# Gated linear unit behind a squared-ReLU attention: fetched and computed key pairs take turns, and v is loaded four key tiles at a time

## The chip, the cores and the metric

The kernel runs on one core of a Trainium2 chip. Its metric is the device time of one execution in microseconds: the median of three runs is 2310.55 us (2309.34 to 2316.06).

## The reference

Eight batches, 3200 rows, 256 columns of `u` and `v`, 64 columns of `z`, all in 32-bit floats.

```python
scores = (1 / S) * z @ z.T                      # per batch, 3200 x 3200
x = u * (maximum(scores, 0) ** 2 @ v)           # 3200 x 256
gate = sigmoid(sum over k < 5 of conv_w[k] * x shifted down by 4 - k rows)
out = (gate * (x @ w_val)) @ w_out
```

The score matrix is symmetric, since both of its factors are `z`. The kernel splits each factor of the large products into a high and a low part and adds three products (low by high, high by low, high by high).

## The kernel before, in words

A batch has 25 key tiles of 128 rows. They are taken in 13 pairs (the last is a single tile), and the queries in 7 chunks of 4, 4, 4, 4, 3, 3, 3 tiles (the last batch: 4, 4, 4, 4, 4, 3, 2). One chunk meets all 13 pairs, one a step; so there are 8 x 7 x 13 = 728 steps. A step at place p of its chunk does, in a fixed order written out by hand (the loop from L919):

- TensorE multiplies the pair's `ah` and `al` (high and low part of the squared scores, transposed) with `vt` into the chunk's two accumulators (`attend`, L552), and forms the scores of the pair three steps ahead (`scores`, L376). A pair product runs as two streams side by side in 64 rows each; where several steps in a row need no scores, it runs over all 128 rows (`attend_whole`, L561).
- The other engines run the work listed for that step (`todo`, filled by `at_step`), then `keep` (L437) sends finished transposes to memory, and `weights_of` (L468) makes the weights of the pair three steps ahead: on ScalarE Relu, Square and the cast to `ah`, on VectorE `al`, the difference.

**Mirrored pairs.** A pair whose scores are the transpose of scores already computed in an earlier chunk isn't computed again. When scores are computed, VectorE transposes them into `turned` (two buffers, L424), and SyncE stores a finished chunk-by-chunk block to memory (`mir`, L446, four transfers). Later `m_fetch` (L450) brings it back, three steps before its weights are made and six before TensorE uses it. Such a fetched pair needs no scores, no Relu, no Square and no transpose. Early chunks have few of them (none in chunk 0, two in chunk 1), late ones many (eleven in chunk 6). `MIRRORED_AT` (L249) says, by the number of fetched pairs in the chunk, which places they take; before, they stand mostly next to each other. A chunk's own second pair is half fetched and half computed and goes last. A pair that spans two query chunks needs two `turned` buffers at once; the last batch has no such pair in its chunks 0 and 1.

**v.** Batch 0 loads v as it goes. For later batches the v of pair i replaces the old one after the last chunk of the batch before has used it. With the step of that use as zero, SyncE issues the load at +3 (four transfers by partition quarter, eight where the pair spans two chunks), ScalarE casts the high part at +6, VectorE subtracts the low part at +7 (L903 to L907). So the last loads and casts fall into chunk 0 of the new batch. `v_raw` has five buffers of one pair, which `z_raw` shares.

**The tail of a chunk.** After place 12 VectorE multiplies the accumulators with `ut`, the transposed u (`gated`, L588; the instruction `x<-acc,ut`, L593). In the following chunk the list `BEHIND` (L823) runs the convolution, the sigmoid, the product with `w_val` (`value`, at step 5 or in pieces over steps that lack scores, L791) and the gating; one chunk later comes the product with `w_out` (`project`), the copies to `ob` and the store (L764). u is loaded by `u_load` (eight transfers a chunk) and transposed by `u_prep` (L582) at the steps of `U_LOAD` and `U_PREP`.

All loads and stores but a few stand in SyncE's queue, in program order: a transfer that must wait holds back all behind it. The same holds for the instructions of each other engine.

## Time and profile before

| | us |
|---|---|
| median of three runs | 2310.55 |
| profiled execution | 2313.36 |
| its span | 2311.6 |
| TensorE matmul busy | 2286.1 (99%) |
| TensorE weight loads busy | 2012.5 (87%) |
| VectorE busy | 1825.2 (79%) |
| ScalarE busy | 1771.8 (77%) |

In the profile PE is TensorE's matmul, PEld its weight load, DVE VectorE, ACT ScalarE, POOL GpSimd and SPq the queue of SyncE. Matmuls are pipelined and their ends are modelled, so a short wait of TensorE can vanish under the matmul before it; a window's length beside that of the same work elsewhere shows it all the same. "[3.62 <-DMA x]" behind a row is the idle time of its engine before it, and what ended it. L-numbers are lines of the kernel.

### The profile page before, as it was taken

What the parts mean: (1) busy time and instruction counts of PE and PEld (TensorE: products, weight loads), DVE (VectorE), ACT (ScalarE), POOL (GpSimd) and SP (SyncE); (2) the same over time, 40 slices, a digit from 0 to 9 for tenths busy, and PEclk for the clock granted to TensorE, in tenths of its full rate; (3) what the DMA queues carried; (4) which work ended last, traced back from release to release, by engine and by line L of the source; (5) the groups of instructions that cost most, each with busy time, mean ns of one, the idle gap of its engine ahead of it and who ended that gap; (6) DMA issues with size and microseconds to landing.
All of it is one profiled execution on the core that took longest, in us unless ns stands there. A gap on an engine that the chain in (4) does not pass through costs nothing.

```text
span 2311.6 us, 53404 instructions
## 1 busy us (share of the span) xinstructions
PE 2286.1 (99%) x21673; PEld 2012.5 (87%) x21673; DVE 1825.2 (79%) x2385; ACT 1771.8 (77%) x2400; POOL 65.5 (3%) x108
## 2 busy tenths in 40 slices
PE   9999999999999999999999999999999999999999
PEld 7889987889888898888988899888998889988889
DVE  7877788787877778887787877878788787888766
ACT  7987778866888668886688866887768877698765
POOL 0000000000000000000000000000000000000000
PEclk9999999999999999999999999999999999999999
DMA  5145676687667776676865777667776676767753
GB/s 123 38 106 129 149 166 149 163 198 191 161 150 170 185 199 158 146 179 167 210 161 138 197 164 198 157 147 197 165 191 153 159 193 156 198 159 189 185 147 101
DMA packets 659639, 375.02 MB, mean 162 GB/s; under 512 B 355520, under 2 KB 630976, under 8 KB 659392
## 3 DMA queue, kind: packets, MB, share of 16 engines
q1 hardware_dynamic: 658192, 371.35, 65.6%
q8 instruction: 169, 2.77, 0.5%
q14 instruction: 78, 0.64, 0.1%
q10 hardware_dynamic: 1200, 0.26, 0.1%
HBM read 205.86 MB, written 165.61 MB: 161 GB/s over the span
## 4 chain that ended last, share of the span: by engine, by line
PE 72%; SPq 7%; DMA 6%; ACT 6%; DVE 6%; issue 3%; DVEq 0%; ACTq 0%
PE acc L350 48%; PE misc L350 8%; PE s L350 7%; PE acc L563 7%; SPq L304 3%; DMA mir<-turned 3%; ACT a L516 2%; DVE al L525 2%; SPq L446 2%; ACT a L517 2%; DVE turned L424 2%; DMA v_raw<-in_v_dram 2%; SPq L168 1%; DMA m<-mir 1%; ACT ah L519 1%
## 5 line engine op out<-in xcount | busy, mean ns | idle before, releaser
L350 PE MATMUL acc<-ah,v_hl 64*128 64x512 f32 (+1 forms) x9656 | 1529.5, 371 | 4.2 <-DVE v_hl L337 3.5
L350 PEld LDWEIGHTS acc<-ah,v_hl 64*128 64x128 f32 x9656 | 907.0, 185 | 135.6 <-ACT ah L519 4.0
L350 PE MATMUL acc<-al,v_hl 64*128 64x512 f32 (+1 forms) x4828 | 911.5, 373 | 13.2 <-DVE al L525 12.6
L525 DVE TENSOR_TENSOR al<-a,ah 128x1024 fp32r<-128x1024 f32 (+3 forms) x387 | 423.1, 1094 | 222.1 <-ACT ah L519 213.2
L350 PEld LDWEIGHTS acc<-al,v_hl 64*128 64x128 f32 x4828 | 458.4, 185 | 90.6 <-DVE al L525 25.6
L525 DVE TENSOR_TENSOR al<-m,ah 128x768 fp32r<-128x768 f32 (+2 forms) x303 | 308.6, 1021 | 102.1 <-ACT ah L519 101.8
L516 ACT ACTIVATE a<-s 128x1024 f32<-128x1024 f32 (+3 forms) x387 | 355.3, 918 | 42.3 <-PE s L350 36.9
L519 ACT CAST ah<-m 128x768 fp32r<-128x768 f32 (+2 forms) x303 | 266.8, 893 | 153.3 <-DMA m<-mir 97.5
L517 ACT ACTIVATE a<-a 128x1024 f32<-128x1024 f32 (+3 forms) x387 | 371.2, 959 | 12.3
L424 DVE STREAM_TRANSPOSE turned<-a 128x1024 f32<-128x1024 f32 (+3 forms) x318 | 319.8, 1011 | 39.0 <-DMA mir<-turned 38.0
L519 ACT CAST ah<-a 128x1024 fp32r<-128x1024 f32 (+3 forms) x352 | 334.8, 951 | 11.2
L634 DVE SCALAR_TENSOR_TENSOR gate<-x,cw,gate 128x512 f32<-128x512 f32 (+2 forms) x448 | 305.2, 681 | 4.4 <-ACT gate L632 0.3
L350 PE MATMUL s<-zq,zhl 64*128 64x512 f32 (+3 forms) x1722 | 234.4, 373 | 1.3 <-ACT zq L231 1.3
L563 PE MATMUL acc<-ah,v_hl 128*128 128x384 f32 (+2 forms) x772 | 196.1, 332 | 0.2 <-DVE x L593 0.2
L350 PEld LDWEIGHTS s<-zq,zhl 64*128 64x128 f32 x1722 | 159.2, 185 | 26.7 <-ACT zq L231 1.6
L696 ACT CAST gvh<-gv 128x512 fp32r<-128x512 f32 (+2 forms) x112 | 64.2, 574 | 123.3 <-DVE gv L692 123.3
L639 ACT ACTIVATE gate<-gate 128x512 f32<-128x512 f32 (+2 forms) x112 | 65.5, 585 | 102.6 <-DVE gate L634 102.1
L563 PEld LDWEIGHTS acc<-ah,v_hl 128*128 128x128 f32 x772 | 137.8, 188 | 4.6 <-issue 1.5
L563 PE MATMUL acc<-al,v_hl 128*128 128x384 f32 (+2 forms) x386 | 127.7, 331 | 0.0
L350 PE MATMUL misc<-w_out_hi,gvl 64*128 64x256 f32 x676 | 98.3, 286 | 0.0
L593 DVE TENSOR_TENSOR x<-acc,ut 128x512 f32<-128x512 f32 (+2 forms) x112 | 65.9, 624 | 39.9 <-PE acc L350 26.2
L350 PE MATMUL misc<-w_out_hi,gvh 64*128 64x256 f32 x676 | 96.1, 279 | 0.0
(119 smaller groups left out, 2019.9 us busy)
## 6 DMA issues: line engine op xcount, KB each, us to landing
m<-mir SPq DMA_DIRECT2D x191, 384.0 KB, 4.7
mir<-turned SPq DMA_DIRECT2D x340, 192.0 KB, 3.5
mir<-turned SPq DMA_DIRECT2D x188, 256.0 KB, 4.3
m<-mir SPq DMA_DIRECT2D x94, 512.0 KB, 6.0
v_raw<-in_v_dram SPq DMA_DIRECT2D x328, 64.0 KB, 2.0
u_raw<-in_u_dram SPq DMA_DIRECT2D x264, 64.0 KB, 2.6
out_dram<-ob SPq DMA_DIRECT2D x33, 512.0 KB, 5.2
mir<-turned SPq DMA_DIRECT2D x84, 144.0 KB, 2.5
```

What stands on the lines that cost most here:

```text
L304: nc.sync.dma_start(dst[a * BLK : (a + 1) * BLK], v[b, k : k + m * BLK, :].rearrange("(t r) d -> r t d", r=BLK))
L350: ins = nc.tensor.matmul(out_, st[r], mv[r], start=first, stop=last)
L424: nc.vector.transpose(into[:, t : t + m], a[:, j * w : (j + m) * w].rearrange("p (t m x) -> p t m x", t=m, x=BLK))
L516: nc.scalar.activation(a.rearrange("p (j x) -> p j x", j=2), s[:, :, :each], AF.Relu, scale=scale)
L517: nc.scalar.activation(a, a, AF.Square)
L519: nc.scalar.copy(hi, a)
L525: nc.vector.tensor_tensor(lo, a, f32(hi), op=ALU.subtract)
L563: nc.tensor.matmul(out_, st, mv, start=first, stop=last)
L593: nc.vector.tensor_tensor(x[:, h, HALO : HALO + w], accs[b, c][h][:, :w], ut[b, c][:, h, :w], op=ALU.mult)
L634: nc.vector.scalar_tensor_tensor(g, tap, cw[:, h, k : k + 1], g, op0=ALU.mult, op1=ALU.add)
L639: nc.scalar.activation(g, g, AF.Sigmoid)
L696: nc.scalar.copy(gvs[b, c][0][:, e, :w], gv_[b, c, e][:, :w])
```

## The change

1. `MIRRORED_AT` puts fetched pairs at every second place where there are few of them, and one at place 1 where there are six, eight or nine. The last place of the chunk goes to a computed pair in three of these.
2. `VALUE_AT` names the places at which `value` is cut into pieces: none for two, four or six fetched pairs (there it runs whole at step 5), three or five places for the rest.
3. v of batches 1 to 7 is loaded in groups of four tiles at the steps of `V_LOAD`, counted from the start of the last chunk of the batch before, and cast at the steps of `V_HIGH` (low part one later). `v_raw` has two buffers of four tiles; `z_raw` has one of its own. A group that spans two chunks takes eight transfers, others four.
4. u of the first chunk is loaded at steps 6 to 9 instead of 2 to 5 and transposed at step 11 instead of 6; u of the second is loaded at steps 12 to 15 instead of 7 to 10, and transposed at 17 instead of 14; that of the third starts at step 18 instead of 15.
5. The small transposes (L434) of chunk 1's first pair go behind the two products `x<-acc,ut` of chunk 0.

```diff
     MIRRORED_AT = {
-        2: (8, 9),
-        4: (7, 8, 9, 10),
-        6: (4, 7, 8, 9, 10, 11),
+        2: (4, 8),
+        4: (4, 6, 8, 10),
+        6: (1, 4, 6, 8, 10, 12),
         7: (4, 5, 7, 8, 9, 10, 11),
-        8: tuple(range(4, 12)),
-        9: tuple(range(4, 13)),
+        8: (1, 4, 5, 6, 7, 8, 9, 11),
+        9: (1, 4, 5, 6, 7, 8, 9, 10, 11),
     }
...
+    def v_load(b, tiles, into=None):
+        raw = sb.tile([P, CW // P, D], F32, name="v_raw", bufs=2) if into is None else into
+        for j, k in enumerate(tiles):
+            v_raw[b, k] = raw, j
+        j = 0
+        while j < len(tiles):
+            g, t = all_homes[b][tiles[j]]
+            m = 1
+            while j + m < len(tiles) and all_homes[b][tiles[j + m]] == (g, t + m):
+                m += 1
+            v_rows(raw[:, j : j + m], b, g, t, m)
+            j += m
...
             if not mirrored(b, c, i):
+                if c == 1 and two_pairs(b, c) and i == own(b, c, 0) and place[b, c, i] == 0:
+                    return lambda: turn(b, c, i, a)
                 turn(b, c, i, a)
...
+    VALUE_AT = {2: (), 4: (), 6: (), 7: (4, 5, 6, 7, 8), 8: (4, 5, 6), 9: (4, 5, 6, 7, 8)}
...
-    U_LOAD = ((-6, -6, -11, -11, -11, -11, -6), (-6, -2, -2, -9, -11, -11, -6))
-    U_PREP = ((1,) * n_chunks, (10, 10, 3) + (1,) * (n_chunks - 3))
+    U_LOAD = ((6, -1, -8, -11, -11, -11, -6), (-6, -2, -2, -9, -11, -11, -6))
+    U_PREP = ((11, 4) + (1,) * (n_chunks - 2), (10, 10, 3) + (1,) * (n_chunks - 3))
+
+    V_LOAD = (
+        (
+            (-1, (0, 1, 2, 3)),
+            (1, (4, 5, 6, 7)),
+            (5, (22, 23)),
+            (7, (8, 9, 10, 11)),
+            (9, (12, 13, 14, 15)),
+            (12, (16, 17, 18, 19)),
+            (14, (20, 21, 24)),
+        ),
+        (
+            (-1, (0, 1, 2, 3)),
+            (1, (4, 5, 6, 7)),
+            (6, (8, 9, 10, 11)),
+            (8, (12, 13, 14, 15)),
+            (10, (16, 17, 18, 19)),
+            (12, (20, 21, 22, 23)),
+            (15, (24,)),
+        ),
+    )
+    V_HIGH = ((3, 4, 4, 6, 10, 11, 12, 13, 14, 15, 16, 8, 17), (3, 4, 5, 6, 8, 9, 10, 11, 12, 13, 14, 15, 17))
...
-            for i in range(NP):
-                free = start(b - 1, n_chunks - 1) + place[b - 1, n_chunks - 1, i]
-                at_step(free + 3, v_load, b, i)
-                at_step(free + 6, v_high, b, i)
-                at_step(free + 7, v_low, b, i)
+            s1 = start(b - 1, n_chunks - 1)
+            for i, p in enumerate(V_HIGH[b > 1]):
+                at_step(s1 + p, v_high, b, i)
+                at_step(s1 + p + 1, v_low, b, i)
+            for p, tiles in V_LOAD[b > 1]:
+                at_step(s1 + p, v_load, b, tiles)
...
                 if p != NP - 2:
-                    while held:
-                        held.pop(0)()
+                    for do in held[:]:
+                        held.remove(do)
+                        after = do()
+                        if after:
+                            held.append(after)
```

The first row of `V_LOAD` and `V_HIGH` is that of batch 1, the second that of batches 2 to 7.

More of the change, by code (lines that the diff above doesn't have):

```diff
@@ L155, in convert @@
         weights[name] = (hi, lo)
-    RAWS = 5
     zt = {}
@@ L177, in z_load @@
         else:
-            raw = sb.tile([P, CW // BLK, BLK], F32, name="z_raw", tag="v_raw", bufs=RAWS)
+            raw = sb.tile([P, CW // BLK, BLK], F32, name="z_raw", bufs=1)
         blocks_load(
@@ L296, in runs @@
         return out_
-    v_two = {}
     def v_rows(dst, b, g, t, m):
@@ L306, in v_rows, with v_load0 @@
             )
-    def by_chunk(b, i):
-        return b == 0 and all(2 <= g < 6 for _, g, _, _ in runs(b, i))
+    def v_load(b, tiles, into=None):
[10 more added lines that the diff above has]
+            j += m
+    two = {}
     def v_load_chunk(b, g):
         if g % 2 == 0:
-            v_two[b, g // 2] = sb.tile([P, 2, CW // P, D], F32, name="v_raws", tag="turned", bufs=2)
-        n = all_sizes[b][g]
-        v_rows(v_two[b, g // 2][:, g % 2, :n], b, g, 0, n)
-    def v_load(b, i):
-        raw = sb.tile([P, 2, D], F32, name="v_raw", bufs=RAWS)
-        v_raw[b, i] = raw
-        for j, g, t, m in runs(b, i):
-            v_rows(raw[:, j : j + m], b, g, t, m)
-    def v_parts(b, i):
-        if by_chunk(b, i):
-            return [(j, m, v_two[b, g // 2][:, g % 2, t : t + m]) for j, g, t, m in runs(b, i)]
-        return [(0, pairs[i][1], v_raw[b, i][:, : pairs[i][1]])]
+            two[0] = sb.tile([P, 2, CW // P, D], F32, name="v_raws", tag="turned", bufs=2)
+        v_load(b, range(all_firsts[b][g], all_firsts[b][g] + all_sizes[b][g]), two[0][:, g % 2])
+    def v_load0(k):
+        if k % 4 == 0 or k == 22:
+            two[1] = sb.tile([P, CW // P, D], F32, name="v_raw", bufs=2)
+        x = k // 2 % 2 if k < 22 else (k - 22) // 2
+        v_load(0, range(k, min(k + 2, NT)), two[1][:, 2 * x : 2 * x + 2])
+    def v_parts(b, i):
+        k, n = pairs[i]
+        if n == 2 and v_raw[b, k][0] is v_raw[b, k + 1][0] and v_raw[b, k][1] + 1 == v_raw[b, k + 1][1]:
+            raw, j = v_raw[b, k]
+            return [(0, 2, raw[:, j : j + 2])]
+        return [(x, 1, v_raw[b, k + x][0][:, v_raw[b, k + x][1] : v_raw[b, k + x][1] + 1]) for x in range(n)]
     def v_high(b, i):
@@ L789, in attn_glu_kernel @@
     }
+    VALUE_AT = {2: (), 4: (), 6: (), 7: (4, 5, 6, 7, 8), 8: (4, 5, 6), 9: (4, 5, 6, 7, 8)}
     def value_places(b, c):
-        s0 = start(b, c)
-        at_ = [p for p in range(4, 9) if lacks(s0 + p)] if (b, c) > (0, 1) and spread(b, c) else []
-        return at_ if len(at_) in PIECES else []
+        if (b, c) < (0, 2) or not spread(b, c):
+            return ()
+        return VALUE_AT.get(sum(mirrored(b, c, i) for i in range(NP)), ())
     def project_places(b, c):
@@ L806, in by_halves @@
         b, c, p = *chunk_of(s), s % NP
-        return p in value_places(b, c) or p in project_places(b, c)
+        return p in value_places(b, c) or p in project_places(b, c) or (p == VALUE and spread(b, c))
     todo = {}
@@ L897, in attn_glu_kernel @@
                 at_step(i - 2 if i else -3, v_low, b, i)
-                if not by_chunk(b, i):
-                    at_step(i - 5, v_load, b, i)
+            for k in (0, 2, 4, 6, 22, 24):
+                at_step(k // 2 - 5, v_load0, k)
             for g in range(2, 6):
@@ L1028, in attn_glu_kernel @@
         project_whole(b, c, spare=True)
-        for x, tag in enumerate(("zz", "v_raw")):
-            ob = sb.tile([P, CW // P * D // 2], F32, name="ob_half", tag=tag, bufs=(1, RAWS)[x])[:, : all_sizes[b][c] * D // 2]
+        for x, tag in enumerate(("zz", "z_raw")):
+            ob = sb.tile([P, CW // P * D // 2], F32, name="ob_half", tag=tag, bufs=1)[:, : all_sizes[b][c] * D // 2]
             (nc.scalar.copy, nc.vector.tensor_copy)[x](ob, pos[b, c][x][:, : all_sizes[b][c] * D // 2])
```

1 row of the table PIECES is left out of this document.

## The prediction

> **What bounds the kernel now.** I read the engine shares first, then the waits, then the busy time of TensorE in windows cut at the ends of chunks (where the first `x<-acc,ut` of a chunk starts).
>
> ```profile
> span 2311.6 us, 53404 instructions
> PE 2286.1 (99%) x21673; PEld 2012.5 (87%) x21673; DVE 1825.2 (79%) x2385; ACT 1771.8 (77%) x2400; POOL 65.5 (3%) x108
> ```
>
> The profiled execution took 2313.36 us, 1.8 us outside its span; the median of the runs, 2310.55 us, lies 2.8 us below it. TensorE is the bound, and the change leaves its work alone: counting through the plan, 303 of the 728 pair steps are fetched before and after, so the same score matmuls are left out, and 725 steps before the closing stretch hold 87 in the 128-row form instead of 93, with 15 changes of form both times. What can move is the time in which TensorE waits. Where that is shows in windows, each sum over seven batches (batches 1 to 7): chunk 0, chunk 1, chunk 4, chunks 5 and 6. After "us" come the window's length and TensorE's busy time in it.
>
> ```profile
> 1450.50:1499.40 48.90, 47.21 (x436) 38.78 (x434) 42.67 (x56) 43.88 (x57) 0.10 (x1) 1.00 0.68 166
> 2021.60:2068.40 46.80, 46.80 (x441) 39.16 (x440) 42.50 (x55) 42.97 (x56) 0.11 (x1) 1.00 0.68 167
> sum 336.60, PE 330.17 PEld 272.00 DVE 299.15 ACT 306.33 POOL 0.73; mean PE 47.17 PEld 38.86 DVE 42.74 ACT 43.76 POOL 0.10
> ...
> 1499.40:1546.90 47.50, 46.62 (x430) 38.12 (x428) 37.41 (x45) 39.53 (x49) 1.42 (x2) 1.00 0.60 148
> 2068.40:2113.80 45.40, 45.40 (x424) 37.88 (x422) 37.41 (x44) 40.61 (x50) 1.41 (x2) 1.00 0.62 155
> sum 329.90, PE 325.18 PEld 266.64 DVE 261.96 ACT 277.87 POOL 9.93; mean PE 46.45 PEld 38.09 DVE 37.42 ACT 39.70 POOL 1.42
> ...
> sum 247.00, PE 245.16 PEld 234.04 DVE 192.51 ACT 160.23 POOL 7.54; mean PE 35.02 PEld 33.44 DVE 27.50 ACT 22.89 POOL 1.08
> ...
> sum 450.70, PE 450.70 PEld 444.26 DVE 356.49 ACT 287.33 POOL 15.40; mean PE 64.39 PEld 63.47 DVE 50.93 ACT 41.05 POOL 2.20
> ```
>
> The last batch does the same matmuls in its chunks 0 and 1 without an idle moment, in 46.80 and 45.40 us. Against that the seven chunks 0 lose 336.60 - 7 x 46.80 = 9.0 us and the chunks 1 lose 329.90 - 7 x 45.40 = 12.1 us. Chunk 4 shows 247.00 - 245.16 = 1.8 us idle, chunks 5 and 6 none. The first batch adds two stalls, each with a drop of the granted clock (the column after POOL):
>
> ```profile
> 40.00:44.00 4.00, 1.34 (x10) 0.87 (x8) 3.23 (x8) 2.31 (x3) 0.00 (x0) 0.81 0.39 71
> 44.00:48.00 4.00, 4.00 (x20) 3.35 (x20) 4.00 (x9) 0.58 (x1) 0.00 (x0) 0.50 0.52 95
> 48.00:52.00 4.00, 4.00 (x35) 3.67 (x33) 1.69 (x5) 3.05 (x4) 0.00 (x0) 0.83 0.67 168
> ...
> 300.00:304.00 4.00, 2.68 (x18) 2.06 (x18) 1.77 (x4) 3.78 (x8) 0.00 (x0) 0.74 0.74 185
> 304.00:308.00 4.00, 4.00 (x40) 3.95 (x40) 3.73 (x7) 3.33 (x6) 0.00 (x0) 0.83 0.61 115
> ```
>
> The first costs 2.66 us of idleness, 4.00 x 0.50 = 2.0 at half clock and 4.00 x 0.17 = 0.7: 5.3 us. The second costs 1.32 + 2.68 x 0.26 + 4.00 x 0.17 = 2.7 us. So some 9.0 + 12.1 + 1.8 + 5.3 + 2.7 = 31 us could be had, and no more from these edits.
>
> **The change part by part.**
>
> **A, first u behind v.** This is the wait behind the stall at 43 us, and under it the transfers with their size and their time from issue to landing:
>
> ```profile
> 40.74 1.25 DVE L582 STREAM_TRANSPOSE ut<-u_raw 128x1024 f32<-128x1024 f32 x1 [3.62 <-DMA u_raw<-in_u_dram]
> ...
> v_raw<-in_v_dram SPq DMA_DIRECT2D x328, 64.0 KB, 2.0
> u_raw<-in_u_dram SPq DMA_DIRECT2D x264, 64.0 KB, 2.6
> v_raws<-in_v_dram SPq DMA_DIRECT2D x8, 128.0 KB, 2.9
> ```
>
> VectorE stood at step 6 for the u of chunk 0, and the v halves and `al` of steps 8 and 9 stood behind it. Now these eight u transfers are issued at steps 6 to 9, behind the v loads, and transposed at step 11; the product that reads them comes after step 12, so two steps of some 3.6 us (46.80 / 13) cover the landing of 2.6 us. Without that cover the wait would move in front of `x<-acc,ut`. I take 5.0 of the 5.3 us; ends 2.7 (the stall goes, the clock still drops) and 5.3.
>
> **B, v of batch 1 earlier.** In chunk 6 of the first batch ScalarE waits for v with the fetched casts queued behind it:
>
> ```profile
> 297.38 0.62 ACT L332 CAST v_hl<-v_raw 128x512 fp32r<-128x512 f32 x1 [3.61 <-DMA v_raw<-in_v_dram]
> ```
>
> The first eight v tiles are now issued at steps -1 and 1 of that chunk, and its last pair is computed, no longer fetched. I take 2.2 of 2.7; ends 0 and 2.7.
>
> **C, v of later batches by four tiles, cast two or three steps sooner.** Per batch 56 v issues become 36 (32 for the last), 288 instead of 432 in all. Chunk 0 of batch 5, SyncE's queue and then VectorE:
>
> ```profile
> 1456.62 5.50 SPq L304 DMA_DIRECT2D v_raw<-in_v_dram  x12
> 1462.21 3.02 SPq L446 DMA_DIRECT2D mir<-turned  x4
> 1465.34 3.14 SPq L304 DMA_DIRECT2D v_raw<-in_v_dram  x4
> 1468.58 0.41 SPq L764 DMA_DIRECT2D out_dram<-ob  x1
> 1469.03 2.75 SPq L304 DMA_DIRECT2D v_raw<-in_v_dram  x4
> 1471.82 4.18 SPq L446 DMA_DIRECT2D mir<-turned  x5
> ...
> 1468.62 1.25 DVE L424 STREAM_TRANSPOSE turned<-a 128x1024 f32<-128x1024 f32 x1 [1.26 <-DMA mir<-turned]
> 1478.38 1.25 DVE L424 STREAM_TRANSPOSE turned<-a 128x1024 f32<-128x1024 f32 x1 [1.88 <-DMA mir<-turned]
> ```
>
> SyncE issues without a pause; the stores of `turned` stand behind v, so their two buffers come free late, and VectorE loses 1.26 + 1.88 = 3.1 us there. An issue costs 5.50 / 12 = 0.46 us. In steps 12 to 15 there were 20 v issues, now 12: the stores go out 8 x 0.46 = 3.7 us sooner, more than the 3.1. Two of the six v casts that fell into chunk 0 move into chunk 6, where TensorE never idles: 2 x 0.618 = 1.2 us off ScalarE and about as much off VectorE.
>
> ```profile
> L332 ACT CAST v_hl<-v_raw 128x512 fp32r<-128x512 f32 x84 | 51.9, 618 | 39.1 <-DMA v_raw<-in_v_dram 39.1
> L516 ACT ACTIVATE a<-s 128x1024 f32<-128x1024 f32 x271 | 276.8, 1022 | 29.2 <-PE s L350 23.9 <-DVE turned L424 5.2
> L517 ACT ACTIVATE a<-a 128x1024 f32<-128x1024 f32 x271 | 287.7, 1062 | 8.6
> L424 DVE STREAM_TRANSPOSE turned<-a 128x1024 f32<-128x1024 f32 x179 | 221.8, 1239 | 20.7 <-DMA mir<-turned 20.5
> ```
>
> Of 9.0 I take 7; ends 2 (the casts alone) and 9.0.
> The Trainium skill (DMA: Bandwidth & Descriptors, section Issuing engines are not separate DMA queues) says that the time to start a transfer is usually small beside the transfer itself. By it the dropped issues would buy nothing, C would be 2 and the sum 14 instead of 19; here the trace disagrees, with twelve issues back to back in 5.50 us and a store waiting behind them.
>
> **D, fetched and computed alternate.** Chunk 1 of batch 5:
>
> ```profile
> 1513.81 1.24 DVE L424 STREAM_TRANSPOSE turned<-a 128x1024 f32<-128x1024 f32 x1
> 1523.96 0.71 DVE L424 STREAM_TRANSPOSE turned<-a 128x512 f32<-128x512 f32 x1 [2.97 <-DMA mir<-turned]
> 1526.01 1.22 DVE L525 TENSOR_TENSOR al<-a,ah 128x1024 fp32r<-128x1024 f32 x1
> ...
> 1516.04 0.41 SPq L764 DMA_DIRECT2D out_dram<-ob  x1
> 1516.49 3.58 SPq L446 DMA_DIRECT2D mir<-turned  x4
> ...
> PEld acc L350 <- DVE al L525: 1.7, 2, 1.3
> ```
>
> The pair that spans two chunks needs a second `turned` buffer, and that one is still on its way to memory; `al` of step 7 comes late, and in this chunk TensorE's weight loads wait for it twice, 1.7 us in all, 1.3 at most. The last batch has no such pair, and no loss. The buffer was full at 1513.81 + 1.24 = 1515.05 but was sent at 1516.49, behind the store of the output. With a fetched pair at place 4 instead of 9 the same three pairs are computed one step later: the store of the output is then already gone (1.4 us won), and before step 7 ScalarE has saved one Relu and Square (1.022 + 1.062 = 2.1 us) and VectorE one transpose (1.24). Together 2.6 us on VectorE against the 1.7. TensorE's work up to step 7 stays the same (five score groups before and after). Of 12.1 I take 8, since ScalarE has spare time only when VectorE is not behind; ends 0 and 12.1. In chunk 4 a fetched pair at place 1 relieves the step that idles: 1 of 1.8, ends 0 and 1.8. In chunks 2 and 3 the value matmuls go back from pieces into step 5, which lacks scores and so has room; nothing is won there, and a stall can appear: -1, ends 0 and -12.1 (as bad as chunk 1 now).
>
> **E, what the four-tile loads cost.** `v_raw` has two buffers of four tiles, so a load waits for the low parts of the previous owner, one step back or in the same step, and is cast two steps on, where it used to be three. Chunk 6 hides ScalarE's waits for v now (39.1 us in all, over seven batches), though not in batch 0. I take -3; ends 0 and 7 x 2.7 = -19. A transfer of 128 KB lands after 2.9 us, one of 64 KB after 2.0. `z_raw` gets a single buffer of its own; every load is at least as late as the transpose before it, so it goes with E.
>
> **F, small transposes behind the gate.**
>
> ```profile
> L434 DVE STREAM_TRANSPOSE turned<-a 128x256 f32<-128x256 f32 x60 | 22.9, 421 | 0.0
> ```
>
> Seven times two small transposes go behind `x<-acc,ut` at the start of chunk 1. The scores and the projection stand between that product and the next use of its banks, so I count nothing; if that cover were gone, they would save 7 x 2 x 0.421 = 5.9 us.
>
> The sum: 5.0 + 2.2 + 7 + 8 + 1 - 1 - 3 = 19.2 us. From the profiled 2313.4 that is 2294.2; from the median 2291.4 us. I forecast 2291.
> The Trainium skill (Perfetto Trace Analysis, section Identifying the Most-Contended Engine) judges TensorE's room by the share of weight loads, not of matmuls; at 87% that would leave 13%, or 299 us, where this text finds 31. The trace does not bear it out: chunk 1 of the last batch has TensorE busy for 45.40 of 45.40 us with weight loads at 37.88, or 83%.
>
> **The rivals.** *The loss moves on inside the chunk.* VectorE and ScalarE are busy for 42.67 and 43.88 us of chunk 0, so when one wait goes, the next step may be late instead. Then C and D give 2 each: 5.0 + 2.2 + 2 + 2 - 1 - 3 = 7.2 us, 2303. Against it stands the last batch, which carries the same work without idling. *No difference beyond the start.* The three pairs of D are still computed in successive steps, so the two buffers collide as before and the alternation doesn't do what it says; with C at its low end spent by E, 5.0 + 2 - 3 - 1 = 3 us, 2307.5. *Slower.* The four-tile loads come two steps ahead of their casts, with SyncE held by a VectorE that trails ScalarE. Where ScalarE then stands for v as long as the 3.61 us above, chunk 6 has no reserve left and TensorE stalls with a drop of the clock, 2.7 us in each of seven batches. That is -19, it uses up C and leaves 4 of D: 5.0 + 4 - 19 - 1 = -11, 2321.5. It decides from a wait of about 3 us per batch; against it, waits that summed to 39.1 us cost nothing in chunks 6.
>
> **How the numbers follow.** The forecast (gains of 9 to 33 us) 0.60; the loss moving on 0.20; no difference 0.12; slower 0.08. About 0.3%, 7 us, is what a measurement can tell from no change. Faster: 0.60 and, since the second case lies near that bound, 0.16 of its 0.20, together 0.76; same: the other 0.04 and the third case, 0.16; slower 0.08. All terms at their best give 5.3 + 2.7 + 9 + 12.1 + 1.8 = 31 us, 2279.6; the range adds a little for small gaps that no row shows, and reaches up past the third case: 2277 to 2308. The forecast's own bounds are 2277 to 2301.
>
> **What would show it.** Right: no 3.62 us wait of `ut` and a full clock from 44 to 52 us; chunks 0 and 1 of batches 1 to 6 at about 47 and 46 us; the wait of `turned` for its stores (38.0 us in total before) down by more than half; v issues 288. Wrong: idle time of TensorE in chunks 6, or a granted clock of 0.5 anywhere after the start (E); chunks 1 still at 47.5 us with the 3 us wait of `turned` in place (D); stalls in chunks 2 and 3.

## The result, and the profile after

The changed kernel takes 2289.97 us (median of four runs, 2285.6 to 2293.92) against 2311.76 us of the kernel before, measured beside it: a ratio of 0.9903, 95% interval 0.9878 to 0.9928. A second measurement gave 0.9892 (0.9878 to 0.9905). The forecast was 2291. The profiled execution took 2285.6 us and was the fastest of the four, so its gain of 27.8 us is larger than the 21.8 us of the medians.

The first lines of the page after, and then windows of the same kind as in the prediction: chunk 0 (batch 5, then the sum over batches 1 to 7), chunk 1 (batch 5, then the sum), chunk 4 (sum), chunks 5 and 6 together (sum).

```profile
span 2283.8 us, 53383 instructions
PE 2271.2 (99%) x21781; PEld 2034.1 (89%) x21781; DVE 1819.7 (80%) x2386; ACT 1774.3 (78%) x2399; POOL 65.9 (3%) x108
```

```profile
1431.20:1476.90 45.70, 44.98 (x413) 37.44 (x411) 40.71 (x52) 43.24 (x55) 0.10 (x1) 1.00 0.68 171
...
sum 319.50, PE 316.72 PEld 280.00 DVE 285.97 ACT 299.90 POOL 0.74; mean PE 45.25 PEld 40.00 DVE 40.85 ACT 42.84 POOL 0.11
...
1476.90:1522.80 45.90, 45.90 (x432) 38.34 (x430) 38.02 (x46) 41.10 (x51) 0.38 (x2) 1.00 0.70 157
sum 321.20, PE 321.20 PEld 272.02 DVE 265.71 ACT 285.05 POOL 2.68; mean PE 45.89 PEld 38.86 DVE 37.96 ACT 40.72 POOL 0.38
...
sum 245.00, PE 245.00 PEld 234.98 DVE 191.14 ACT 156.63 POOL 6.82; mean PE 35.00 PEld 33.57 DVE 27.31 ACT 22.38 POOL 0.97
...
sum 461.40, PE 460.73 PEld 451.28 DVE 360.94 ACT 296.77 POOL 17.67; mean PE 65.82 PEld 64.47 DVE 51.56 ACT 42.40 POOL 2.52
```

Chunks 1 went from 329.90 to 321.20 us and chunks 4 from 247.00 to 245.00, both now without an idle moment of TensorE. Chunks 0 went from 336.60 to 319.50, while chunks 5 and 6 grew from 450.70 to 461.40. That growth is mostly no loss. With the new places six score matmuls of each batch have moved, by way of the chunks between, from chunk 2 to chunk 5 (54 and 6 in the trace before, 48 and 12 after), about 1 us per batch. And `x<-acc,ut`, which ends a window, now comes late at the end of chunk 6, so that some of chunk 0's products count for chunk 6. For this reason the experiments below take chunk 6 together with the chunk 0 that follows.

The waits of the changed kernel (engine, line and what it waited for: us in total, times, longest):

```profile
ACT a L529 <- PE s L363: 130.9, 82, 4.3
ACT ah L532 <- DMA m<-mir: 54.9, 49, 4.5
ACT v_hl L345 <- DMA v_raw<-in_v_dram: 38.4, 39, 3.7
DVE turned L437 <- DMA mir<-turned: 5.9, 8, 1.7
PEld acc L363 <- DVE x L608: 4.8, 6, 1.8
```

The wait of `turned` for its stores fell from 38.0 to 5.9 us. ScalarE's wait for scores rose from 36.9 to 130.9, and the wait of TensorE's weight loads for `al` (L525, now L538) fell from 25.6 to 0.8: the other engines now wait for TensorE and no longer the other way round. But the wait of the v casts stayed (39.1, now 38.4), and a new wait of TensorE stands at the start of some chunks 0. This is the largest, at the start of the last batch (start, length, engine and line; in brackets the idle time before it):

```profile
1987.66 0.62 ACT L345 CAST v_hl<-v_raw 128x512 fp32r<-128x512 f32 x1 [1.53 <-DMA v_raw<-in_v_dram]
...
1993.79 0.69 DVE L534 CAST ah<-a 128x1024 fp32r<-128x1024 f32 x1
...
1994.39 1.02 DVE L608 TENSOR_TENSOR x<-acc,ut 128x384 f32<-128x384 f32 x2
...
1995.46 0.19 PEld L363 LDWEIGHTS acc<-ah,v_hl 64*128 64x128 f32 x2 [1.82 <-DVE x L608]
```

ScalarE waits 1.53 us for v in chunk 6, everything behind it comes later, VectorE's cast of `ah` stands ahead of `x`, and TensorE needs the accumulators that `x` sets free. In the first batch the stall at 302 us has only moved: TensorE now waits 2.3 us for `gvl` (the low part of the gated values, an operand of the product with `w_out`) at 304.95.

### The profile page after: what moved, and what is told of

It reads as the page before. It is cut to its first block, busy times and chain, and to the rows that moved or that the text cites. A ratio compares the mean times of both kernels' runs of the same rounds, so it can differ in the third digit from the quotient of the medians.

```text
span 2283.8 us, 53383 instructions
## 1 busy us (share of the span) xinstructions
PE 2271.2 (99%) x21781; PEld 2034.1 (89%) x21781; DVE 1819.7 (80%) x2386; ACT 1774.3 (78%) x2399; POOL 65.9 (3%) x108
## 4 chain that ended last, share of the span: by engine, by line
PE 92%; DMA 3%; DVE 2%; SPq 1%; ACT 1%; issue 1%; DVEq 0%; ACTq 0%
PE acc L363 65%; PE s L363 10%; PE misc L363 10%; PE acc L578 6%; DMA v_raw<-in_v_dram 2%; SPq L166 1%; DMA z_raw<-in_z_dram 1%; PE misc L749 1%; PE misc L694 1%; SPq L300 0%; DVE al L538 0%; ACT a L529 0%; ACT a L530 0%; DMA m<-mir 0%; DVE v_hl L350 0%
## 5 line engine op out<-in xcount | busy, mean ns | idle before, releaser
L363 PE MATMUL acc<-ah,v_hl 64*128 64x512 f32 (+1 forms) x9800 | 1552.7, 369 | 3.6 <-DVE x L608 3.3
L363 PEld LDWEIGHTS acc<-ah,v_hl 64*128 64x128 f32 x9800 | 937.5, 184 | 124.0 <-DVE x L608 4.8
L363 PE MATMUL acc<-al,v_hl 64*128 64x512 f32 (+1 forms) x4900 | 930.2, 369 | 0.2
L538 DVE TENSOR_TENSOR al<-a,ah 128x1024 fp32r<-128x1024 f32 (+3 forms) x387 | 423.1, 1094 | 253.8 <-ACT ah L532 246.6
L363 PEld LDWEIGHTS acc<-al,v_hl 64*128 64x128 f32 x4900 | 476.7, 184 | 57.0 <-DVE al L538 0.8
L529 ACT ACTIVATE a<-s 128x1024 f32<-128x1024 f32 (+3 forms) x387 | 355.4, 918 | 140.9 <-PE s L363 130.9
L532 ACT CAST ah<-m 128x768 fp32r<-128x768 f32 (+2 forms) x303 | 269.0, 893 | 111.3 <-DMA m<-mir 54.9
L538 DVE TENSOR_TENSOR al<-m,ah 128x768 fp32r<-128x768 f32 (+2 forms) x303 | 308.7, 1021 | 53.3 <-ACT ah L532 52.9
L363 PEld LDWEIGHTS s<-zq,zhl 64*128 64x128 f32 x1722 | 162.2, 184 | 21.3 <-ACT zq L229 0.4
L578 PE MATMUL acc<-ah,v_hl 128*128 128x384 f32 (+2 forms) x700 | 177.6, 331 | 0.2 <-DVE x L608 0.2
L578 PEld LDWEIGHTS acc<-ah,v_hl 128*128 128x128 f32 x700 | 124.7, 188 | 4.7 <-issue 1.1
L578 PE MATMUL acc<-al,v_hl 128*128 128x384 f32 (+2 forms) x350 | 115.5, 330 | 0.0
```

The lines of the kernel that those rows point to most:

```text
L363: ins = nc.tensor.matmul(out_, st[r], mv[r], start=first, stop=last)
L529: nc.scalar.activation(a.rearrange("p (j x) -> p j x", j=2), s[:, :, :each], AF.Relu, scale=scale)
L532: nc.scalar.copy(hi, a)
L538: nc.vector.tensor_tensor(lo, a, f32(hi), op=ALU.subtract)
L578: nc.tensor.matmul(out_, st, mv, start=first, stop=last)
```

## The experiments

All runs in one table. The second column is the difference of the median to the kernel before, measured on the same chip; the others are worked out from the profiled executions, as the time from the first `x<-acc,ut` of a chunk to that of the next: chunk 1 alone, and chunks 1 to 5, summed over batches 1 to 7; and chunk 6 with the chunk 0 behind it, summed over the seven places where they meet.

| kernel | to before, us | chunk 1 | chunks 1 to 5 | chunks 6 and 0 |
|---|---|---|---|---|
| before | 0 | 329.9 | 1415.3 | 587.2 |
| after | -21.8 | 321.2 | 1408.4 | 572.9 |
| after, once more | -25.3 | 321.2 | 1408.4 | 573.6 |
| old places | -10.3 | 335.5 | 1423.1 | 576.5 |
| old u | -17.4 | 321.2 | 1408.0 | 580.7 |
| old v | -19.1 | 321.2 | 1408.2 | 580.7 |
| new places in chunk 1 only | -20.9 | 321.2 | 1409.2 | 579.6 |
| fetched pairs side by side | -22.2 | 323.3 | 1410.2 | 576.3 |
| v by two tiles | -1.6 | 321.2 | 1408.0 | 598.4 |
| small transposes late in chunk 0 too | -6.9 | 321.2 | 1408.4 | 592.7 |
| small transposes all at once | -20.3 | 321.0 | 1408.3 | 581.5 |
| v by chunk | -22.4 | 321.6 | 1408.6 | 578.1 |
| v by chunk, a step later | -23.8 | 321.6 | 1408.5 | 575.7 |
| late transposes and later v | -19.2 | 321.2 | 1408.5 | 579.8 |

Two things can be read at once. Wherever chunk 1 has its new places, chunks 1 to 5 take 1408 to 1410 us, whatever else is changed. Among these kernels all other differences lie where chunk 6 meets chunk 0, apart from the first chunk of old u.

Two cautions go with the table. The profiled executions scatter at these meeting places: in the two of the changed kernel the first of them, behind the first batch, takes 83.3 and 86.4 us. And the windows are cut at `x<-acc,ut`, an instruction of VectorE, so they also measure how late VectorE is at the cut. TensorE's own first product with `w_out` in each chunk (`misc<-w_out_hi,gvl`) stands at a fixed place of its work. Cut there, the same sums are:

| kernel | chunk 1 | chunks 1 to 5 | chunks 6 and 0 |
|---|---|---|---|
| before | 330.3 | 1425.7 | 577.4 |
| after | 320.8 | 1411.5 | 570.3 |
| after, once more | 320.8 | 1411.6 | 571.0 |
| old places | 331.9 | 1429.3 | 570.7 |
| old v | 320.8 | 1411.4 | 578.1 |

The gain of all together is the same, but by this cut two thirds of it lie in chunks 1 to 5 and not where chunks 6 and 0 meet.

### The changed kernel again, and its three parts taken back

> The changed kernel once more, beside the three that take back one part each: 2290 us, some 21.8 us (0.94%) below the kernel before. It is the zero from which the three others are counted.

Measured: 2289.11 against 2314.43, 25.3 us less. The next three kernels ran on the same chip and are counted from it.

**Old places** (D).

```diff
-                at_ = MIRRORED_AT[len(fetched)]
+                at_ = (MIRRORED_AT if b == 0 and c == n_chunks - 1 else OLD_AT)[len(fetched)]
...
-    VALUE_AT = {2: (), 4: (), 6: (), 7: (4, 5, 6, 7, 8), 8: (4, 5, 6), 9: (4, 5, 6, 7, 8)}
+    VALUE_AT = {2: (5, 6), 4: (4, 5, 6, 7), 6: (4, 5, 6, 7, 8), 7: (4, 5, 6, 7, 8), 8: (4, 5, 6, 7, 8), 9: (4, 5, 6, 7, 8)}
```

> The changed kernel, but the fetched pairs stand at the old places and the value matmuls come in the old pieces (chunk 6 of the first batch alone keeps the new places). Theory (D, the alternation, is worth 8 us): 8 us slower than the changed kernel, 2298; chunks 1 of batches 1 to 6 take about 47 us instead of 45.9, and the waits of `turned` for its stores rise from 5.9 us towards 20. Rival 1 (the loss moves on, D gives 2 or less): within 2 us of the changed kernel, 2290 to 2292, chunks 1 at 46. Rival 2 (D carries nearly all of it, and C needs D): 15 us or more slower, 2305.

Measured: 2304.13 (ratio 0.9961, 0.9948 to 0.9973), 15.0 us above the changed kernel: the size of rival 2, though not its second half, that C needs D (below). The collision is there as the prediction told it. From its waits, its windows of chunk 1 (the sum), SyncE's queue and VectorE in chunk 1 of batch 5 (in one stretch of time):

```profile
DVE turned L446 <- DMA mir<-turned: 22.7, 16, 3.1
```

```profile
sum 335.40, PE 329.22 PEld 271.61 DVE 266.07 ACT 274.99 POOL 2.65; mean PE 47.03 PEld 38.80 DVE 38.01 ACT 39.28 POOL 0.38
```

```profile
1508.87 0.41 SPq L788 DMA_DIRECT2D out_dram<-ob  x1
1509.32 3.56 SPq L468 DMA_DIRECT2D mir<-turned  x4
...
1516.57 0.71 DVE L446 STREAM_TRANSPOSE turned<-a 128x512 f32<-128x512 f32 x1 [2.74 <-DMA mir<-turned]
```

The first buffer goes out behind the store of the output, and the transpose of the spanning pair waits 2.74 us for it. Chunks 1 take 335.4 us here, 5.5 us more than in the kernel before, but most of that is the cut. These are TensorE's first product with `w_out` and VectorE's `x` at the start of chunk 1 of batch 5, in the kernel before and then here:

```profile
1498.59 0.28 PE L350 MATMUL misc<-w_out_hi,gvl 64*128 64x256 f32 x2
1499.38 1.25 DVE L593 TENSOR_TENSOR x<-acc,ut 128x512 f32<-128x512 f32 x2
...
1491.08 0.28 PE L372 MATMUL misc<-w_out_hi,gvl 64*128 64x256 f32 x2
1491.28 1.29 DVE L617 TENSOR_TENSOR x<-acc,ut 128x512 f32<-128x512 f32 x2
```

VectorE comes to `x` 0.79 us after TensorE's product before, and 0.20 us here, so the window opens sooner. Cut at TensorE's product, chunks 1 differ by 1.6 us (330.3 and 331.9) and chunks 1 to 5 by 3.6, in one profile of each. So at most a part of what the new v gains is passed on as a loss, and the collision costs about what it cost before.

**Old u** (A).

```diff
-    U_LOAD = ((6, -1, -8, -11, -11, -11, -6), (-6, -2, -2, -9, -11, -11, -6))
-    U_PREP = ((11, 4) + (1,) * (n_chunks - 2), (10, 10, 3) + (1,) * (n_chunks - 3))
+    U_LOAD = ((-6, -6, -11, -11, -11, -11, -6), (-6, -2, -2, -9, -11, -11, -6))
+    U_PREP = ((1,) * n_chunks, (10, 10, 3) + (1,) * (n_chunks - 3))
```

> The changed kernel, but the u of the first chunk is fetched and transposed at the old steps. Theory (A is worth 5.0 us): 5 us slower than the changed kernel, 2295; `ut` waits about 3.6 us for `u_raw` near 41 us, TensorE idles 2.7 us there and the granted clock falls to 0.5 behind it. Rival 1 (the idle time goes, the clock would have fallen anyway, A = 2.7): 2 to 3 us slower. Rival 2 (the new v loads alone move the wait away, since fewer issues stand behind u): no difference over 1 us and no wait of `ut`.

Measured: 2297.03 (0.993, 0.9917 to 0.9943), 7.9 us above. VectorE, TensorE's weight loads, then windows of this kernel, and then windows of the changed kernel:

```profile
40.45 1.25 DVE L597 STREAM_TRANSPOSE ut<-u_raw 128x1024 f32<-128x1024 f32 x1 [3.35 <-DMA v_raw<-in_v_dram]
...
42.85 0.22 PEld L363 LDWEIGHTS acc<-ah,v_hl 64*128 64x128 f32 x2 [2.70 <-ACT ah L532]
```

```profile
44.00:46.00 2.00, 2.00 (x13) 1.76 (x11) 2.00 (x7) 0.00 (x0) 0.00 (x0) 0.50 0.40 81
46.00:48.00 2.00, 2.00 (x15) 1.80 (x13) 1.97 (x5) 1.73 (x2) 0.00 (x0) 0.66 0.76 127
```

```profile
40.00:44.00 4.00, 4.00 (x40) 3.23 (x37) 3.27 (x8) 3.66 (x5) 0.00 (x0) 1.00 0.51 100
44.00:48.00 4.00, 4.00 (x42) 3.35 (x39) 2.97 (x8) 3.75 (x5) 0.00 (x0) 1.00 0.30 111
```

The wait of `ut` is back (the row names a transfer of v as what ended it, not u), and with it the stall and the half clock. The first chunk ends 4.0 us later (at 60.3 instead of 56.3 us). That is what A is worth in its place. The other 3.9 us lie where chunks 6 and 0 meet (580.7 against 573.6), in code that is the same in both kernels. There the kernel with all small transposes at once (581.5) is as far from the changed one, and both profiles have a drop of the clock (at 1160 and at 874 us) that neither profile of the changed kernel has. The intervals of the two ratios leave room for a difference as small as 2.8 us. Whether A acts that far isn't shown.

**Old v** (B, C, E).

```diff
-        raw = sb.tile([P, CW // P, D], F32, name="v_raw", bufs=2) if into is None else into
+        raw = sb.tile([P, 2, D], F32, name="v_raw", bufs=RAWS)
...
-            for p, tiles in V_LOAD[b > 1]:
-                at_step(s1 + p, v_load, b, tiles)
+                at_step(free + 3, v_load, b, i)
+                at_step(free + 6, v_high, b, i)
+                at_step(free + 7, v_low, b, i)
```

> The changed kernel, but v of every batch is fetched, cast and split pair by pair at the old steps, with five buffers of two tiles. Theory (B 2.2 + C 7 - E 3): 6 us slower than the changed kernel, 2296; `turned` waits again for its stores for over 20 us in all, chunks 0 of batches 1 to 6 take about 47.5 us instead of 45.6, and TensorE idles 1.3 us again near 302 us. Rival 1 (E eats C, as the wait of the v casts is still 38.4 us): within 2 us, with the stalls of TensorE at the start of chunks 0 of batches 3, 5 and 7 (1.15, 0.88, 1.77 us) gone. Rival 2 (v carries most of the gain): 12 us or more slower.

Measured: 2295.31 (0.9918, 0.9904 to 0.9931), 6.2 us above, as the terms had it. Three of its waits:

```profile
ACT v_hl L332 <- DMA v_raw<-in_v_dram: 37.9, 31, 3.1
ACT ah L519 <- DMA m<-mir: 36.3, 21, 3.5
DVE turned L424 <- DMA mir<-turned: 19.4, 17, 2.4
```

The waits of `turned` are 13.5 us longer than in the changed kernel, TensorE's weight loads wait 11.8 us for `al` (0.8 and 2.6 in the two profiles of the changed kernel), and chunks 0 take 334.3 instead of 319.4 us: C is real. But the wait of the v casts is the same with either scheme (37.9 and 38.4). What the new scheme makes longer is the wait of `ah` for the fetched `m`, from 36.3 to 54.9 us, as the v loads now stand between the fetches of chunk 6. Chunks 6 take 253.5 instead of 246.4 us to the late `x` at their end. TensorE itself loses nothing inside them: from its first product with `w_out` to that of the next chunk, chunks 6 of batches 1 to 6 take 33.5 us each in the kernel before, in this one and in the changed one. E is paid at the start of chunk 0, where TensorE's weight loads wait for `x`: 1.4 us in all here, 4.8 and 2.3 in the two profiles of the changed kernel. At the end of batch 0 this kernel's weight loads wait 1.4 us for `gvl` and 1.2 us for `x`, the changed kernel's 2.3 us for `gvl`.

### What of D counts

**New places in chunk 1 only.** The kernel with the old places, but its rows for two fetched pairs are the new ones.

```diff
     OLD_AT = {
-        2: (8, 9),
+        2: (4, 8),
...
-    VALUE_AT = {2: (5, 6), 4: (4, 5, 6, 7), 6: (4, 5, 6, 7, 8), 7: (4, 5, 6, 7, 8), 8: (4, 5, 6, 7, 8), 9: (4, 5, 6, 7, 8)}
+    VALUE_AT = {2: (), 4: (4, 5, 6, 7), 6: (4, 5, 6, 7, 8), 7: (4, 5, 6, 7, 8), 8: (4, 5, 6, 7, 8), 9: (4, 5, 6, 7, 8)}
```

> The kernel with the old places (2304.1 us, 15.0 us over the changed kernel), but chunk 1 alone has its two fetched pairs at the new places 4 and 8 and its value matmuls whole. Theory (what D is worth lies in chunk 1): the seven chunks 1 come back from 48.2 to 45.9 us, 7 x 2.3 = 16 us less some for the start of chunk 2, so 10 to 15 us faster than with the old places, 2289 to 2294. Rival (the backlog is handed from chunk to chunk, and chunks 2 to 4 need the new places too): chunks 1 at 46, but chunks 2 and 4 lose a microsecond each, 7 us or less won, 2297 or more.

Measured: 2291.87, 20.9 us below before (0.9906, 0.9894 to 0.9919), 1 to 4 us above the changed kernel, which can't be told from nothing. Chunks 1 are at 45.9 us. Chunks 2 and 4 take 5.1 and 2.8 us more than in the changed kernel, but chunk 5 takes 6.5 us less, since the scores stay where they were. Of the 15.0 us of D, chunk 1 alone brings 10.6 back (from 10.3 to 20.9 us below before).

**Fetched pairs side by side.**

```diff
     MIRRORED_AT = {
-        2: (4, 8),
+        2: (4, 5),
```

> The changed kernel, but the two fetched pairs of chunk 1 stand side by side at places 4 and 5 instead of 4 and 8. Theory of the prediction (what counts is one fetched pair at place 4, so that the pair that spans two chunks comes when its buffer is free): within 2 us of the changed kernel, 2289 to 2291, chunks 1 at 45.9 to 46.1. Rival (what counts is that no more than three computed pairs stand in a row, so that ScalarE and VectorE catch up): seven computed pairs in a row from place 6 run late, chunks 1 at 47 to 48, 7 to 14 us slower, 2296 to 2303.

Measured: 2290.57, 22.2 us below before (0.9902, 0.9889 to 0.9915), the same as the changed kernel; `turned` waits 4.2 us for its stores, chunks 1 take 46.2 us. So it isn't the alternation. One fetched pair at place 4 and one right behind it are enough, ahead of the pair that spans two chunks.

### What of v counts

**v by two tiles.**

```diff
-            while j + m < len(tiles) and all_homes[b][tiles[j + m]] == (g, t + m):
+            while m < (2 if b else 4) and j + m < len(tiles) and all_homes[b][tiles[j + m]] == (g, t + m):
```

> The changed kernel, but the v of batches 1 to 7 is fetched by at most two tiles in one transfer, at the same steps into the same buffers: 52 to 56 issues per batch instead of 36. Theory (an issue holds SyncE's queue for 0.46 us, and the stores of `turned` stand behind it): the waits of `turned` for its stores rise from 5.9 us to 15 or more, chunks 0 take half a microsecond to one more, 3 to 7 us slower, 2292 to 2296. Rival 1, by the rule that the time to start a transfer is small beside the transfer: within 1 us, 2289 to 2290. Rival 2 (the long landing of 4.4 us of a four-tile transfer is what makes ScalarE wait for v): the waits of the v casts fall from 38 us to 20, the stalls at the start of the chunks 0 go, 2 us faster.

Measured: 2311.25, 1.6 us below before (0.9992, 0.9983 to 1.0): 20 us or more slower than the changed kernel, far beyond all three expectations. SyncE's queue in chunk 6 of batch 2 (the number at the end counts the issues), ScalarE, the waits, and the sum of the windows of chunk 6 (236.30 in the changed kernel); then SyncE's queue of the changed kernel at the same place:

```profile
838.13 1.21 SPq L474 DMA_DIRECT2D m<-mir  x2
839.39 5.27 SPq L300 DMA_DIRECT2D v_raw<-in_v_dram  x8
844.76 1.77 SPq L474 DMA_DIRECT2D m<-mir  x2
846.59 4.84 SPq L300 DMA_DIRECT2D v_raw<-in_v_dram  x8
...
859.76 0.83 ACT L532 CAST ah<-m 128x768 fp32r<-128x768 f32 x1 [2.93 <-DMA m<-mir]
```

```profile
ACT ah L532 <- DMA m<-mir: 84.0, 52, 3.5
DVE turned L437 <- DMA mir<-turned: 2.7, 5, 1.2
```

```profile
sum 254.30, PE 243.10 PEld 232.79 DVE 197.90 ACT 154.59 POOL 9.47; mean PE 34.73 PEld 33.26 DVE 28.27 ACT 22.08 POOL 1.35
```

```profile
834.48 1.21 SPq L474 DMA_DIRECT2D m<-mir  x2
835.74 2.04 SPq L300 DMA_DIRECT2D v_raw<-in_v_dram  x4
837.88 1.20 SPq L474 DMA_DIRECT2D m<-mir  x2
839.12 2.62 SPq L300 DMA_DIRECT2D v_raw<-in_v_dram  x4
```

The issue is the price, as the theory had it, but not where it had it: `turned` waits less than in the changed kernel, and it is the fetches of `m` between the v loads of chunk 6 that come late, 84.0 instead of 54.9 us of waits, and TensorE idles there and at the start of chunk 0. There the clock takes a part of the 20 us. At the starts of chunks 0 of batches 4 to 7 the granted clock falls to one half for 3.41 us, which neither profile of the changed kernel shows; this is the first of the four:

```profile
1162.56:1165.97 3.41, 3.41 (x20) 2.74 (x18) 3.38 (x5) 3.08 (x6) 0.00 (x0) 0.50 0.48 110
```

Four of them are 4 x 3.41 x 0.50 = 6.8 us of TensorE's work. The same two-tile transfers at the old steps (old v) cost 6 us; at the new steps they cost 20. Without the larger transfers the earlier steps would have eaten nearly the whole gain.
The Trainium skill (DMA: Bandwidth & Descriptors, section Issuing engines are not separate DMA queues) calls the time to start a transfer usually small beside the transfer itself; by it this run would have shown no difference. The trace doesn't agree: the same bytes in 144 transfers more took 20 us longer, with eight issues holding the queue for 5.27 us ahead of a fetch.

**v by chunk, and a step later.** In batches 2 to 6 no load spans two chunks: 28 issues instead of 36. In the second kernel the last two loads and their casts come a step later, behind the first stores of chunk 0 (the last lines of the diff).

```diff
+    BY_CHUNK = (
...
+        (10, (16, 17, 18)),
+        (12, (19, 20, 21)),
+        (15, (22, 23, 24)),
+    )
...
-        (12, (19, 20, 21)),
-        (15, (22, 23, 24)),
+        (13, (19, 20, 21)),
+        (16, (22, 23, 24)),
```

> The changed kernel, but in batches 2 to 6 the last three loads of v hold the tiles 16 to 18, 19 to 21 and 22 to 24, so that none spans two chunks: 28 issues per batch instead of 36, eight fewer behind the fetches of chunk 6, at the same steps. Theory (each issue less on SyncE's queue brings the fetches of `m` and the stores of `turned` forward; 20 more of them cost 20 us over seven batches, 0.14 us each): up to 40 x 0.14 = 5.7 us faster, I expect 1 to 5, 2284 to 2288; the waits of `ah` for `m` fall below 50 us and the stalls at the starts of chunks 0 halve. Rival 1 (the price of an issue is only seen above some number of them): within 1 us. Rival 2 (three transfers of three tiles need the v buffers later than before, and casts come a step later): slower by 1 us or more.

> As the kernel before in this list, but the last two loads come one step later, behind the first stores of `turned` of chunk 0 instead of ahead of them, with their casts one step later too. Theory (the order of stores and v loads on SyncE's queue decides, as where the delayed small transposes put the stores behind v and lost 15 us): the stores of the first pairs of chunk 0 go out some 2 us sooner; `turned` waits less than 5.9 us in all; 0 to 2 us faster than with the earlier steps. Rival (the casts that move into chunk 0 take ScalarE's spare time there): chunks 0 at 46 to 47 us instead of 45.6, 2 to 8 us slower.

Measured: 22.4 us (0.9904, 0.9887 to 0.992) and 23.8 us (0.9902, 0.9884 to 0.9919) below before. Both are the changed kernel's time. In the second the waits of `turned` fall to 1.1 us, but those of `ah` for `m` stay at 56.8. Eight issues fewer per batch buy nothing, where some 20 more per batch cost 20 us: from 36 issues down to 28 nothing more is won.

### The small transposes

**All at once** (F).

```diff
-                if c == 1 and two_pairs(b, c) and i == own(b, c, 0) and place[b, c, i] == 0:
+                if False and two_pairs(b, c) and i == own(b, c, 0) and place[b, c, i] == 0:
```

> The changed kernel, but the two small transposes of the first pair of chunk 1 come at once again, ahead of `x<-acc,ut`. Theory (F is worth nothing, since scores and projection cover the product): within 1 us of the changed kernel, chunks 1 at 45.9 us. Rival 1 (that cover is gone now that the chunks run without idle time): x and the first product of chunk 1 come 0.84 us later at each of seven starts, up to 5.9 us slower, with TensorE idle at the starts of chunks 1. Rival 2 (as in chunk 0, stores that go out earlier are the better order): 1 us or more faster.

Measured: 2292.71, 20.3 us below before (0.9914, 0.9899 to 0.9929). That is 1 to 5 us slower than the changed kernel; the intervals overlap, and chunks 1, where F acts, take 321.0 us without it and 321.2 us with it. F is worth nothing that these runs can tell.

**Late in chunk 0 too.** I meant this to beat the changed kernel: the two transposes stand ahead of `x` at the stalls shown above.

```diff
-                if c == 1 and two_pairs(b, c) and i == own(b, c, 0) and place[b, c, i] == 0:
+                if c < 2 and two_pairs(b, c) and i == own(b, c, 0) and place[b, c, i] == 0:
```

> The changed kernel, but the two small transposes of the first pair of chunk 0 wait behind `x<-acc,ut` too, as the change has it for chunk 1. Theory (VectorE runs late there and the first product of chunk 0 waits for it: 1.15, 0.88 and 1.77 us in the profile of the changed kernel): x comes 0.84 us sooner at each start, the stalls at the starts of chunks 0 (3.8 us in all) halve, 1 to 3 us faster, 2286 to 2288. Rival 1 (another instruction is what is late, a v cast of ScalarE or the low part): within 1 us. Rival 2 (the stores of these transposes come later and their readers wait): 1 us or more slower, with longer waits of `ah` for `m`.

Measured: 2305.88, 6.9 us below before (0.9968, 0.9955 to 0.998): 15 us or more lost. SyncE's queue, VectorE and TensorE at the start of batch 1, and the waits:

```profile
311.64 3.79 SPq L300 DMA_DIRECT2D v_raw<-in_v_dram  x8
315.48 6.51 SPq L459 DMA_DIRECT2D mir<-turned  x8
...
320.50 1.25 DVE L437 STREAM_TRANSPOSE turned<-a 128x1024 f32<-128x1024 f32 x1 [3.90 <-DMA mir<-turned]
...
324.84 0.50 PE L363 MATMUL acc<-al,v_hl 64*128 64x512 f32 x2 [3.28 <-DVE al L538]
```

```profile
DVE turned L437 <- DMA mir<-turned: 20.7, 13, 3.9
```

The transposes moved by 0.8 us, but their four stores moved behind eight v issues. The stores of the next block queue up behind those, VectorE waits 3.90 us for a buffer, `al` comes late, TensorE idles 3.28 us.

**Late transposes and later v** undoes that: the v load of step 12 comes at step 13 in every batch, behind these stores. It stands on top of the second kernel by chunk, whose 28 issues and later steps changed nothing by themselves.

> The kernel with the small transposes of chunk 0 behind `x<-acc,ut` too (2305.9 us), but the v load that stood ahead of their stores on SyncE's queue comes one step later, behind them (step 13 instead of 12 in every batch, its casts a step later too; batches 2 to 6 with 28 issues as in the late kernel, 2289.3 us). Theory (the 15 us came from the stores that fell behind eight v issues of 0.46 us, so that `turned` waited 20.7 us): the waits of `turned` for its stores are 6 us or less again and chunks 0 take 45.6 us without a stall at their steps 4; the transposes now leave x free 0.84 us sooner, so the stalls at the starts of chunks 0 and in chunk 6 of batch 0 (5 to 7 us in all) shrink: 2284 to 2289. Rival 1 (the transposes themselves, now in a busier place on VectorE, cost the 15 us): 2300 or more, chunks 0 at 47 us or more again. Rival 2 (stores a step later make the fetch of these blocks late): waits of `ah` for `m` above 65 us, 2292 to 2298.

Measured: 2292.31, 19.2 us below before (0.9911, 0.9898 to 0.9925). 12 of the 15 us are back and `turned` waits 1.3 us instead of 20.7, so the order on SyncE's queue was the cause of most of the loss. It still doesn't beat the changed kernel: TensorE's weight loads wait 8.1 us for `al` (0.8 and 2.6 in the changed kernel). What makes `al` late there was not followed further. No kernel of this study is faster than the changed one.

## Why the prediction was right, and where not

The forecast was 2291 with a sum of 19.2 us; measured were 21.8 and 25.3 us of gain. The time was right. One term failed in its mechanism (B), one in its place (E), and one was too small by half (D). That the sum came so near is in part luck: D brought more than its 8 us, and a B that hangs on the clock was counted in full.

**A, 5.0 us.** Taken back alone it shows 4.0 us in its place; the first chunk of the changed kernel ends 5.6 us sooner than that of the kernel before. Right, and the wait and the half clock were the ones named.

**B, 2.2 us.** Its mechanism is not borne out. The stall at 302 us became a wait of 2.3 us for `gvl` at 304.95, and with the old v loads the same place loses 1.4 + 1.2 us. The step that failed is that ScalarE's wait for v was all that stood there; VectorE, with the small transposes ahead of `gvl`, was next. Nor is the drop of the clock there gone (0.74 in the kernel before): the profile shown has a clock of 1.00 behind that wait, but in the second profile of the same kernel the same wait, 2.3 us, is followed by half clock (rows at the end). Cut at TensorE's products, chunk 6 of batch 0 with the chunk 0 behind it takes 87.3 us before, 87.5 with old v, and 83.4 and 86.5 in the two profiles of the changed kernel: 3.9 or 0.8 us won, and which of the two an execution gets is luck. A granted clock of 0.5 after the start was named as a sign against E; this one stems from the stall for `gvl`, not from E.

**C, 7, and E, -3.** Together with B 6.2 us, and taking v back costs 6.2 us by the medians. In windows cut at `x` chunks 0 win 14.9 us and chunks 6 lose 7.1, but most of both is the late `x` that ends the window. In TensorE's own time chunks 6 lose nothing, and the waits for `x` at the start of chunks 0 are 1 to 3 us longer, near the 3 of E. So C with B is some 7 to 9 us, an estimate, beside the 9.2 of the forecast; that 6.2 was met to the tenth is luck. C's step, that the stores of `turned` go out sooner, is shown by their waits (19.4 to 5.9 us). E's step failed in its place: the prediction looked for it at the v casts, whose waits did not change, and it is at the fetches of `m` (36.3 to 54.9 us), the transfers that the v loads were moved past. The prediction counted the issues that the stores are spared and not those that the fetches get ahead of them. The run by two tiles shows how near this came to no gain at all: with some 20 issues more per batch only 1.6 us of the whole gain are left.

**D, 8 (+1 - 1 in chunks 2 to 4).** Taken back it costs 15.0 us, 10.6 of it in chunk 1. The mechanism was right, down to the place: a fetched pair at place 4, ahead of the spanning pair. What gave the change its name, the alternation, was not needed. The size was off by half. In chunk 1 the prediction took 8 of 12.1 us for fear that VectorE trails; chunk 1 then ran without any idle time. The rest, some 4 us, would lie in chunks 2 to 5, which the prediction had at nil. That is open: by the table they changed by 1.8 us to the worse (1085.4 to 1087.2), cut at TensorE's products by 4.6 to the better (1095.4 to 1090.7), and the kernel with new places in chunk 1 only can't be told from the changed one.

D does not need the new v: old v is 19.1 us below before, of which A accounts for 4.0 in its place, and 15.1 are left. And v and D add up: taken back singly they cost 6.2 + 15.0 = 21.2 us, and all of the change less A's 4.0 is 25.3 - 4.0 = 21.3. Taking back all three singly costs more, 29.1 us, only by the 3.9 us of old u that stay unexplained.

**F, 0.** Right within what could be measured.

Of the rivals, *the loss moves on* had C and D at 2 us each, and *no difference beyond the start* had less. Taken back singly, v (B, C and E) costs 6.2 us and D 15.0, so neither describes the change. *Slower* did not come about in the changed kernel: the new stalls of TensorE at the start of chunks 0 (1.20, 0.93 and 1.82 us before its weight loads in the profile) are the kind it named, but after the first batch the longest wait of a v cast is 2.3 us in one profile and 3.0 in the other, no more than the 3 us from which it was to decide, and no clock dropped there. The run by two tiles shows it in full, with four drops and no gain, though by the waits for `m` and not for v.

## What to carry to other kernels

A step that is moved on a full queue is paid for by what it is moved past: list, for each issue, which fetch and which store it now stands ahead of, in every stage it enters and not only in the one it leaves. A window cut at an instruction of an engine that may be late measures that lateness too: cut it at work of the engine that bounds the kernel before a gain is given to one stage or the other. And an edit of 0.8 us on one engine (two small transposes) can cost 15 us when it changes the order of stores on another.
